# Turning output rows by a VectorE transpose of channel pairs, in a kernel of two attentions on one core

## The chip, the cores and the metric

The kernel runs on one NeuronCore of a Trainium2 chip. The metric is the time of one execution on the device, in microseconds (us), as the median of three runs. One further execution was recorded by the hardware profiler; its page and trace are what the document reads. Engines are named as the profile does: PE is TensorE's matmuls and PEld its loads of the stationary operand, DVE is VectorE, ACT is ScalarE, POOL is GpSimd, and SP issues the DMAs.

## What is computed

The input x has 2048 tokens of 512 channels. Two attentions run over it, and a gate g, one number for each token, mixes them.

```python
g = _sigmoid((x * gate_w).sum(-1, keepdims=True))
a = _A_ref(x, A_mem0, A_Wq, A_Wk, A_Wv, A_Wo, A_seg_len)
b = _B_ref(x, B_wq, B_wk, B_wv, B_wo, B_beta)
return g * a + (1 - g) * b
```

Branch A is a recurrence over 64 segments of 32 tokens. Eight memory rows stand in front of each segment; the 40 rows go through a masked attention with 32 heads of 128, and the output's first eight rows are the memory of the next segment.

```python
for s in range(n_seg):
    h = jnp.concatenate([mem, xs], axis=1)          # 8 + 32 rows
    q, k, v = (einsum('btd,dhe->bhte', h, W) for W in (Wq, Wk, Wv))
    p = _softmax(where(mask, q @ k.T * scale, -1e9))
    o = einsum('bhte,hed->btd', p @ v, Wo)
    mem = o[:, :M, :].copy()
    outs.append(o[:, M:, :])
```

Branch B is an attention with 32 heads of 16 over four chunks of 512 tokens, with a running memory matrix, and an output projection `wo`.

## The kernel before

The program is recorded first and emitted afterwards. `P.op` and `P.dma` append an instruction to an engine's list together with the named resources that it reads and writes, and each engine then runs its list in order and waits by semaphore for the other engines' last writers and readers of those resources. DMAs are all issued by SP, in the order in which they were recorded. So a place in the recording is a place in every queue.

At the start, `plan_loads` brings in x, the three weights of branch B (`wkB`, `wqB`, `wvB`, each 512 x 512 in four blocks of 128 channels), some small inputs, and the large weights of A. `x_chunk` turns x by identity matmuls on TensorE (line 573) into `xT`, channels on partitions. `gate_parts` turns the gate's weights by one more identity matmul (line 605) and computes g. Branch B's projections run in these first 50 us; its last chunk's projections come later, in small portions (`LateB`), with weight chunks loaded again by `ldc`.

After that `plan_a` runs sixteen groups of four segments. The order of the work in each group is written out by hand, in sixteen lists of tokens (`A_LIST0` to `A_LIST15`). `2.K0x` is a unit of segment 2, `bS`, `bE`, `bP`, `bT` are steps of branch B's attention, and units of the group before (`ol...`, `of`) and of still earlier groups (`tb`, `tf`) are mixed in. A tilde swaps ScalarE and VectorE for that copy, and a token with an `e` behind it is the copy that belongs to the unit. The projections are on line 1281, the scores on 1545 and 1550, the softmax sums on 1580, the values on 1610 and 1622, the output projection on 1368.

The output projection leaves four partial sums on four blocks of 32 partitions, in the f32 tile `WF` (`LNF` for the left-over rows). `fold` (line 1386) adds and turns them at once: a stationary operand of 32 channels from `WF` against a matrix `fold` of four stacked identities gives channels on partitions and tokens on columns. Of its result the first eight columns go to `hT` (the memory of the next segment, `hm`), and the others to the staging tile `aT_st` (`w_rows`, unit `ax`). Eight rows of each segment cannot be computed in the recurrence's place and come a group later: `ol_units` projects them, folds them (`of`) and copies them into `aT_st` as well (`ofe`). There are two such tiles, used by turns (`par`).

When a group's tile is whole, one DMA on line 1434 stores it to a scratch tensor `aTd` in DRAM, with channels still on partitions. Later `tail_units` loads it again into `aTg` (line 1452; the token `tl` issues the load once the store is recorded and branch B's rows are there). The unit `tb` projects branch B's rows (line 1463) and ScalarE scales them into `t1_sb`. The unit `tf` turns the reloaded rows by sixteen identity matmuls of 32 x 128 into a PSUM bank (line 1485), and its second half `tfe` has VectorE multiply by the gate, add `t1_sb` (line 1494) and SP store the output (line 1496). The last group skips scratch and is turned straight out of `aT_st`.

## Time and profile before

| what | value |
|---|---|
| median of three runs | 840.78 us (839.33 to 842.3) |
| the profiled execution's own time | 839.92 us |
| its span, from first to last instruction | 837.9 us |
| TensorE clock granted in it | 0.999 of full |
| packets moved, and of them under 512 B | 84442, 55296 |
| line 1485, ident x aTg, 240 matmuls | 6.3 us busy |
| line 1494, scale and add, 128 x 512, 15 times | 741 ns each |
| store of a group's rows (line 1434), 15 times | 128 KB, 1.8 us to landing |
| reload (line 1452), 15 times | 128 KB, 2.1 us to landing |
| output store (line 1496), 15 times | 128 KB, 1.9 us to landing |
| a group of four segments | some 48 us |

The span is what the profile shows of an execution; the time is 2 us longer than it, for what lies around it. A group row of the profile reads: line, engine, operation, tile written and tiles read, shapes, count; then busy time and the mean of one in ns; then the time that the engine was idle just before them, and what ended that. A timeline row reads: start, length, engine, line, operation, and in brackets the idle time before it and what ended it. Matmuls overlap with one another, so a row's length holds a drain that lies under the next work; the distance from start to start is what they cost.

### The profile page before, as it was taken

To read this page: it belongs to the slowest core of one execution; us is meant where nothing else is said; L and a number is where in the kernel's file an instruction comes from. 1 tells how busy PE (TensorE), PEld (TensorE's weight loads), DVE (VectorE), ACT (ScalarE), POOL (GpSimd) and SP (SyncE) were. 2 spreads that over 40 slices of the span, in tenths; PEclk is the share of its full clock that TensorE was granted. 3 is DMA by queue.
4 is the path that set the end of the run, shared out by engine and by line. 5 is a ranking of instruction groups with operands and counts; after the bars stand their busy time and mean duration, and the time that the engine had idled before them with its cause. 6 is when DMAs were issued, how large, how long until landed. Compare 5 with 4: busy or idle time off the path is not lost.

```text
span 837.9 us, 49436 instructions
## 1 busy us (share of the span) xinstructions
PE 808.7 (97%) x22174; PEld 438.8 (52%) x22174; DVE 572.1 (68%) x1381; ACT 589.7 (70%) x1506; POOL 284.6 (34%) x780
## 2 busy tenths in 40 slices
PE   8988999999999999999999999999999999999997
PEld 4544455555555555555555555555655555555554
DVE  4554656677676767766766767878688787777764
ACT  5546777677777777777687677677766677777544
POOL 3613233333333333333342333333333233434110
PEclk9999999999999999999999999999999999999999
DMA  9998212112011120111011020111112011110111
GB/s 318 419 362 243 62 41 61 47 31 62 16 30 41 25 55 27 46 38 46 23 46 39 24 56 25 47 39 40 35 25 61 17 49 32 40 41 15 30 41 47
DMA packets 84442, 57.50 MB, mean 69 GB/s; under 512 B 55296, under 2 KB 79112, under 8 KB 82696
## 3 DMA queue, kind: packets, MB, share of 16 engines
q1 hardware_dynamic: 84232, 54.36, 21.4%
q8 instruction: 174, 2.85, 1.4%
q14 instruction: 36, 0.29, 0.1%
HBM read 37.14 MB, written 17.20 MB: 65 GB/s over the span
## 4 chain that ended last, share of the span: by engine, by line
PE 87%; ACT 6%; DMA 3%; DVE 2%; issue 1%; SPq 1%; DVEq 0%; POOL 0%
PE ps L1281 46%; PE ps L1368 17%; PE ps L1386 3%; PE ps L1610 3%; PE ps L678 2%; PE ps L909 2%; PE ps L962 2%; PE ps L1463 2%; PE ps L1545 2%; PE ps L1580 1%; PE ps L696 1%; ACT PT L930 1%; ACT R_sb L1590 1%; ACT WF L390 1%; DMA wqB<-in_B_wq_dram 1%
## 5 line engine op out<-in xcount | busy, mean ns | idle before, releaser
L936 POOL TENSOR_SCALAR_AFFINE_SELECT PT<-PT 128x128 bf16<-128x128 bf16 (+2 forms) x320 | 117.5, 367 | 202.1 <-ACT PT L930 153.7
L930 ACT ACTIVATE PT<-ps 128x512 bf16<-128x512 f32 x320 | 174.9, 610 | 5.3 <-PE ps L909 4.2
L1281 PE MATMUL ps<-Wv_sb,hT 128*32 128x512 bf16 x2048 | 138.1, 379 | 0.0
L1281 PE MATMUL ps<-Wq_sb,hT 128*32 128x512 bf16 x2048 | 136.3, 379 | 0.4
L1281 PE MATMUL ps<-Wk_sb,hT 128*32 128x512 bf16 x2048 | 135.7, 379 | 0.5
L1368 PE MATMUL ps<-Wo_sb,OT_sb 128*32 128x512 bf16 x2048 | 129.5, 380 | 1.0 <-ACT OT_sb L390 0.6
L1600 POOL TENSOR_TENSOR P_sb<-P_sb,R_sb 128x64 bf16<-128x64 bf16 x128 | 51.0, 398 | 137.0 <-ACT R_sb L1590 131.2
L390 ACT ACTIVATE OT_sb<-ps 128x320 bf16<-128x320 f32 x170 | 68.6, 435 | 22.4 <-PE ps L1622 21.1
L1281 PEld LDWEIGHTS ps<-Wq_sb,hT 128*32 128x32 bf16 x2048 | 58.5, 97 | 46.6 <-ACT hT L390 2.9
L1281 PEld LDWEIGHTS ps<-Wk_sb,hT 128*32 128x32 bf16 x2048 | 58.8, 97 | 45.5 <-ACT hT L390 2.2
L390 ACT ACTIVATE WF<-ps 128x256 f32<-128x256 f32 x105 | 35.2, 381 | 55.3 <-PE ps L1368 53.0
L1368 PEld LDWEIGHTS ps<-Wo_sb,OT_sb 128*32 128x32 bf16 x2048 | 48.2, 96 | 45.5 <-ACT OT_sb L390 7.5
L1293 DVE STREAM_TRANSPOSE KT_sb<-KN_sb 128x256 f32<-128x256 f32 x128 | 56.5, 441 | 22.0 <-ACT KN_sb L390 19.0
L1293 DVE STREAM_TRANSPOSE QT_sb<-QN_sb 128x256 f32<-128x256 f32 x128 | 56.4, 441 | 21.8 <-ACT QN_sb L390 18.2
L390 ACT ACTIVATE QN_sb<-ps 128x512 bf16<-128x512 f32 x78 | 46.9, 604 | 33.3 <-PE ps L1281 32.7
L390 ACT ACTIVATE KN_sb<-ps 128x512 bf16<-128x512 f32 x75 | 45.0, 602 | 31.9 <-PE ps L1281 31.5
L1559 ACT ACTIVATE P_sb<-ps 128x224 bf16<-128x224 f32 x128 | 45.9, 359 | 28.5 <-PE ps L1550 20.4
L1281 PEld LDWEIGHTS ps<-Wv_sb,hT 128*32 128x32 bf16 x2048 | 50.0, 95 | 23.9 <-issue 0.6
L1594 DVE TENSOR_TENSOR P_sb<-P_sb,R_sb 128x160 bf16<-128x160 bf16 x128 | 42.3, 331 | 20.7 <-ACT R_sb L1590 18.5
L392 DVE CAST V_sb<-ps 128x512 bf16<-128x512 f32 x76 | 51.8, 682 | 5.5 <-PE ps L1281 5.1
L392 DVE CAST OT_sb<-ps 128x320 bf16<-128x320 f32 x86 | 41.1, 487 | 18.9 <-PE ps L1622 18.1
L1610 PEld LDWEIGHTS ps<-P_sb,V_sb 32*128 32x128 bf16 x2048 | 23.3, 91 | 57.5 <-DVE P_sb L1594 25.2
(142 smaller groups left out, 1488.6 us busy)
## 6 DMA issues: line engine op xcount, KB each, us to landing
Wk_sb<-in_A_Wk_dram SPq DMA_DIRECT2D x4, 1024.0 KB, 8.9
Wq_sb<-in_A_Wq_dram SPq DMA_DIRECT2D x4, 1024.0 KB, 12.4
Wv_sb<-in_A_Wv_dram SPq DMA_DIRECT2D x4, 1024.0 KB, 15.1
Wo_sb<-in_A_Wo_dram SPq DMA_DIRECT2D x8, 512.0 KB, 5.8
scr_vld<-VNL SPq DMA_DIRECT2D x16, 256.0 KB, 2.8
VL<-scr_vld SPq DMA_DIRECT2D x64, 64.0 KB, 2.6
scr_kqd<-stgk SPq DMA_DIRECT2D x12, 256.0 KB, 9.7
Vj<-scr_vd SPq DMA_DIRECT2D x32, 68.0 KB, 2.4
```

The costliest lines, as they stand in the source:

```text
L390: P.op("act", lambda a: a.activation(dst, src, ACT.Copy), reads=[v.rbank[k] for k in bks], writes=dres, name=name)
L392: P.op("dve", lambda d: d.tensor_copy(dst, src), reads=[v.rbank[k] for k in bks], writes=dres, name=name)
L930: P.op("act", lambda a: a.activation(pt, v.pb[bk], ACT.Exp, scale=v.SCALE_B), reads=[v.rbank[bk]], writes=[rp], name="be%d_%d" % (n, t))
L936: P.op("gp", lambda g: g.affine_select(mv, mv, [[0, len(cut)], [1, 128]], ALU.is_ge, 0.0, base=0, channel_multiplier=-1), reads=[rp], writ ...
L1281: ins = pe.matmul(pb[bk][SEG * j:SEG * (j + 1), :], lhs(c), cols(w, j) if split else w[:, 512 * j:512 * (j + 1)], start=(c == 0), stop=(c ...
L1293: P.op("dve", lambda d: d.transpose(to, src), reads=reads, writes=writes, name=name)
L1368: ins = pe.matmul(pb[bk][SEG * j:SEG * (j + 1), :], lhs(4 * k + j), Wo_sb[:, 4 * k + j, :], start=(first and k == ks[0]), stop=False, skip ...
L1386: ins = pe.matmul(pb[bk][SEG * j:SEG * (j + 1), SEG * n:SEG * (n + 1)], part[:, o:o + SEG], v.fold[:, :], start=True, stop=True, skip_grou ...
L1559: P.op("act", lambda a: a.activation(P_sb[:, b, :], pb[bk][:, 0:224], ACT.Exp, scale=SCALE), reads=[rbank[bk]], writes=[Rs("P%d" % b), Rs( ...
L1594: P.op("dve", lambda d: d.tensor_tensor(wide(P_sb, b)[:, :, 0:L], wide(P_sb, b)[:, :, 0:L], R_sb[:, b, :].rearrange("p (i q) -> p i q", q= ...
L1600: P.op(ENG["n"], lambda d: d.tensor_tensor(left(P_sb), left(P_sb), grp04(R_sb[:, b, :]), ALU.mult), reads=[Rs("R%d" % b)], writes=[Rs("P%d ...
L1610: ins = pe.matmul(pb[bks[j]][:, L * i:L * (i + 1)], V_sb[SEG * j:SEG * (j + 1), b, i * E:(i + 1) * E], P_sb[SEG * j:SEG * (j + 1), b, LW * ...
```

## The change

The rows of a group are now turned before they are stored. VectorE's transpose works on blocks of 32 x 32 words of 32 bits; a word here is a pair of neighbouring channels in bf16. For this the two channels of a pair have to lie beside each other in `aT_st`, so the assignment of channels to partitions changes in the whole kernel: partition p of block (h, n) now holds channel 256 h + 2 p + n instead of 128 c + p. What follows from that:

- B's weights are loaded in pieces of 2 KB (two neighbouring rows), A's weights with every second row to a block, and the weight chunks of `LateB` by two DMAs each.
- The gate's weights come straight into their place by a DMA of 256 pieces of 4 bytes; their turn on TensorE and its copy are gone. The load is issued behind x, and the gate's parts start two steps later.
- The identity matmuls that turn x and the first memory, and the fold, read their stationary operand with a step of two elements (`by_pairs`).
- The copies into `aT_st` write with a step of two bf16 elements (`a_rows`).

A new step `turn` stands where a new token `os` stands in the lists, once for each of the fifteen groups that go through scratch. It transposes the tile in place, and stores it with tokens on the rows by four DMAs, one for each block of 32 partitions, in pieces of 128 B. The store was recorded in `ofe` before; `os` stands some tokens behind it, in most cases near the start of the next list. Apart from `os`, the lists are the same. The reload brings rows of 1 KB with tokens on partitions, the identity matmuls of `tf` are gone for these fifteen groups, and line 1494 reads the reloaded tile in SBUF in place of a PSUM bank, and writes over it. The bank is still taken and given back. The last group keeps its sixteen matmuls, which now read with a step of two and write PSUM with a step of two.

```diff
-    dram("aTd", [NG, 128, C, 128])
+    dram("aTd", [NG, 128, DM])
...
-        ld("b" + nm, dst[:, :, :], src.rearrange("(c p) n -> p c n", p=128), nm + "B", "dma_" + nm)
+        ld("b" + nm, dst[:, :, :].rearrange("p (h n) m -> p h (n m)", h=2), src.rearrange("(h p n) m -> p h (n m)", h=2, n=2), nm + "B", "dma_" + nm)
...
+    P.dma(P.group("gw"), lambda s: s.dma_start(v.gw_sb[:, :].rearrange("p (h n) -> p h n", h=2), gate_w.rearrange("(h p n) -> p h n", h=2, n=2)), writes=[Rs("gw")], name="dma_gwr")
...
+class Pairs:
+    def __init__(self, ap):
+        self.ap = ap.rearrange("p (h t n) -> p h n t", h=2, n=2)
+
+    def __getitem__(self, key):
+        return self.ap[key[0], key[1] // 2, key[1] % 2, key[2]]
+
+
+def by_pairs(ap):
+    return Pairs(ap)
...
-                ins = pe.transpose(v.pb16[bk][:, o:o + 128], v.x_sb[:, i, c * 128:(c + 1) * 128], v.ident[:, :])
+                ins = pe.transpose(v.pb16[bk][:, o:o + 128], by_pairs(v.x_sb[:, i, :])[:, c, :], v.ident[:, :])
...
-    def weights():
-        bk = BK.take()
-        P.op("pe", lambda pe, bk=bk: pe.transpose(v.pb16[bk][:, 0:C], v.gwr_sb[0:C, :], v.ident[0:C, 0:C]),
...
+        for h in range(2):
+            P.dma(grp, lambda s, h=h: s.dma_start(dst[:, h], src[:, h]), writes=[Rs("woc%d" % (i % 4))] + ([Rs("wvB")] if i < 4 else []), name="ldc%d_%d" % (i, h))
...
-                    o = 256 * hf + 128 * n + SEG * j
-                    ins = pe.matmul(pb[bk][SEG * j:SEG * (j + 1), SEG * n:SEG * (n + 1)], part[:, o:o + SEG], v.fold[:, :],
+                    cols = by_pairs(part[:, :])[:, 2 * hf + n, SEG * j:SEG * (j + 1)]
+                    ins = pe.matmul(pb[bk][SEG * j:SEG * (j + 1), SEG * n:SEG * (n + 1)], cols, v.fold[:, :],
...
+    def a_rows(t):
+        return t[:, :, :].rearrange("p c t -> p (c t)").rearrange("p (a t c) -> p a t c", a=2, c=2)
...
-            stored.append(g)
-            P.dma(P.group("as%d" % g, "as%d" % par), lambda sp: sp.dma_start(v.aTd[g], aT_st[par][:, :, :]),
-                  reads=[Rs("aTl%d" % par)] + [Rs("aTx%d_%d" % (par, r)) for r in range(4)], writes=[Rs("aTd%d" % g)], name="sta%d" % g)
+            turns.append(turn)
+
+        def turn():
+            stored.append(g)
+            flat = aT_st[par][:, :, :].rearrange("p c t -> p (c t)")
+            turned = [Rs("aTl%d" % par)] + [Rs("aTx%d_%d" % (par, r)) for r in range(4)]
+            P.op("dve", lambda d: d.transpose(flat.bitcast(F32), flat.bitcast(F32)), writes=turned, name="aT%d" % g)
+            grp = P.group("as%d" % g, "as%d" % par)
+            rows = v.aTd[g].rearrange("(b t) (h j i) -> j t h b i", b=4, h=2, j=4)
+            for j in range(4):
+                P.dma(grp, lambda sp, j=j: sp.dma_start(rows[j], flat[SEG * j:SEG * (j + 1), :].rearrange("p (h b i) -> p h b i", h=2, b=4)),
+                      reads=turned, writes=[Rs("aTd%d" % g)], name="sta%d_%d" % (g, j))
...
             bk = B.take()
+            if not last:
+                return lambda: uf2(bk)
...
-                        ins = pe.matmul(pb[bk][q, c * 128:(c + 1) * 128], rows[:, c, q], ident[:, :], start=True, stop=True)
+                        ins = pe.matmul(by_pairs(pb[bk][q, :])[:, c, :], rows[:, c // 2, q, c % 2], ident[:, :], start=True, stop=True)
...
-                P.op("dve", lambda dv, c=c: dv.scalar_tensor_tensor(fin[:, c], pb[bk][:, c], g_sb[:, g:g + 1], t1_sb[:, c], ALU.mult, ALU.add),
+                P.op("dve", lambda dv, c=c: dv.scalar_tensor_tensor(fin[:, c], (pb[bk] if last else fin)[:, c], g_sb[:, g:g + 1], t1_sb[:, c], ALU.mult, ALU.add),
...
-            dst = aT_st[par][:, :, SEG * r:SEG * (r + 1) - M].rearrange("p (a c) t -> p a c t", a=2)
+            dst = a_rows(aT_st[par])[:, :, SEG * r:SEG * (r + 1) - M, :].rearrange("p a t c -> p a c t")
...
-    common = {"wl": wo_next, "bS": b_s, "bE": b_e, "bP": b_p, "bT": lambda: bat.run_late(1), "pj": late.project, "pp": late.finish}
+    common = {"wl": wo_next, "bS": b_s, "bE": b_e, "bP": b_p, "bT": lambda: bat.run_late(1), "pj": late.project, "pp": late.finish, "os": lambda: turns and turns.pop(0)()}
```

More of the change, by code (lines that the diff above doesn't have):

```diff
@@ L368, in over @@
     def over(home):
-        parts = {"mem0_sb": "mem0", "gwr_sb": "gwr", "beta_sb": "beta", "gB_sb": "gB", "omgB_sb": "omgB"}
+        parts = {"mem0_sb": "mem0", "beta_sb": "beta", "gB_sb": "gB", "omgB_sb": "omgB"}
         ops = []
@@ L415, in build @@
             v.late_const()
-        if n >= 36 and n % 2 == 0 and gates:
+        if n >= 38 and n % 2 == 0 and gates:
             gates.pop(0)()
@@ L601, in gate_parts @@
     st = {}
-    def weights():
-        bk = BK.take()
-        P.op("pe", lambda pe, bk=bk: pe.transpose(v.pb16[bk][:, 0:C], v.gwr_sb[0:C, :], v.ident[0:C, 0:C]),
-             reads=[Rs("gwr"), Rs("ident")], writes=[v.rbank[bk]], name="gwtr")
-        v.evac("dve", v.gw_sb[:, :], v.pb16[bk][:, 0:C], [bk], [Rs("gw")], "gwev")
-        BK.give(bk)
     def dots(k):
@@ L632, in f_m0tr @@
             for c in range(C):
-                ins = pe.transpose(v.pb16[bk][:, c * v.M:(c + 1) * v.M], v.mem0_sb[0:v.M, c * 128:(c + 1) * 128], v.ident[0:v.M, 0:v.M])
+                ins = pe.transpose(v.pb16[bk][:, c * v.M:(c + 1) * v.M], by_pairs(v.mem0_sb[0:v.M, :])[:, c, :], v.ident[0:v.M, 0:v.M])
             return ins
@@ L637, in memory @@
         BK.give(bk)
-    return [weights, memory] + [lambda k=k: dots(k) for k in range(NTT // 4)]
+    return [memory] + [lambda k=k: dots(k) for k in range(NTT // 4)]
 def b_projections(v):
@@ L1446, in tail_units @@
         last = g == ngrp - 1
-        rows = aT_st[g % 2] if last else aTg
+        rows = a_rows(aT_st[g % 2])
         rr = [Rs("aTl%d" % (g % 2))] + [Rs("aTx%d_%d" % (g % 2, r)) for r in range(4)] if last else [Rs("aTg")]
@@ L1451, in tail_units @@
         if not last:
-            P.dma(P.group("al%d" % g, "al"), lambda sp: sp.dma_start(aTg[:, :, :], v.aTd[g]), reads=[Rs("aTd%d" % g)], writes=[Rs("aTg")],
+            P.dma(P.group("al%d" % g, "al"), lambda sp: sp.dma_start(aTg[:, :, :].rearrange("p c t -> p (c t)"), v.aTd[g]), reads=[Rs("aTd%d" % g)], writes=[Rs("aTg")],
                   name="lda%d" % g, scratch=True)
@@ L1493, in uf2 @@
                 c = slice(h * 512 // n, (h + 1) * 512 // n)
[L1494 to L1495 removed]
+                P.op("dve", lambda dv, c=c: dv.scalar_tensor_tensor(fin[:, c], (pb[bk] if last else fin)[:, c], g_sb[:, g:g + 1], t1_sb[:, c], ALU.mult, ALU.add),
+                     reads=([rbank[bk]] if last else [Rs("aTg")]) + [Rs("g"), Rs("t1")], writes=([Rs("aTg")] if not h else []) + ([Rs("aTg%d" % h)] if n > 1 else []), name="fin%d_%d" % (g, h))
                 P.dma(g_out[g], lambda sp, c=c: sp.dma_start(out2d[g * 128:(g + 1) * 128, c], fin[:, c]), reads=[Rs("aTg%d" % h if n > 1 else "aTg")],
@@ L1700, in segment @@
         return units
-    stored, ended, pend = [], [], {}
+    stored, ended, pend, turns = [], [], {}, []
     st = {"tails": 0}
@@ L1795, in plan_a @@
         bat.run_late()
+        assert not turns
         while st["tails"] < ngrp or tail or pend:
```

142 lines of the change are left out of this document (70 added, 72 removed).

## The prediction

> **What bounds the kernel now.** I read the page's first and second parts, then the chain of waits, then every place in the timeline where the removed matmuls run.
>
> ```profile
> PE 808.7 (97%) x22174; PEld 438.8 (52%) x22174; DVE 572.1 (68%) x1381; ACT 589.7 (70%) x1506; POOL 284.6 (34%) x780
> ...
> DMA  9998212112011120111011020111112011110111
> GB/s 318 419 362 243 62 41 61 47 31 62 16 30 41 25 55 27 46 38 46 23 46 39 24 56 25 47 39 40 35 25 61 17 49 32 40 41 15 30 41 47
> ...
> PE 87%; ACT 6%; DMA 3%; DVE 2%; issue 1%; SPq 1%; DVEq 0%; POOL 0%
> ```
>
> TensorE is busy 97% of the span and is 87% of the chain that ends last, so work taken from it can shorten the span. DMA is full only in the first four slices of 21 us. VectorE has a third of the span free. The groups that the edit touches:
>
> ```profile
> L1386 PE MATMUL ps<-fold,WF 128*32 128x32 f32 x2048 | 36.9, 199 | 4.4 <-ACT WF L390 2.1 <-ACT hT L390 0.7 <-DVE oTt L986 0.2
> ...
> L1293 DVE STREAM_TRANSPOSE KT_sb<-KN_sb 128x256 f32<-128x256 f32 x128 | 56.5, 441 | 22.0 <-ACT KN_sb L390 19.0
> ...
> L1545 PEld LDWEIGHTS ps<-QT_sb,KT_sb 128*32 128x32 bf16 x2048 | 31.9, 95 | 28.3 <-DVE QT_sb L1293 10.8 <-DVE KT_sb L1293 8.0 <-issue 1.2
> ...
> L1386 PEld LDWEIGHTS ps<-fold,WF 128*32 128x32 f32 x2048 | 30.7, 111 | 21.5 <-ACT WF L390 8.8 <-DVE WF L392 2.0 <-ACT aT_st L390 1.3
> L1485 PE MATMUL ps<-ident,aTg 128*32 128x128 bf16 x240 | 6.3, 219 | 0.3 <-issue 0.3
> ```
>
> (busy us and mean ns, then idle before). The 240 matmuls of L1485 are what goes; the 6.3 us counts drains that lie under the next work. Start to next start is what counts, and what follows:
>
> ```profile
> 414.63 0.40 PE L1485 MATMUL ps<-ident,aTg 128*32 128x128 bf16 x16
> 414.96 0.27 PE L1610 MATMUL ps<-P_sb,V_sb 32*128 32x40 bf16 x16
> ...
> 808.49 0.40 PE L1485 MATMUL ps<-ident,aTg 128*32 128x128 bf16 x16
> 809.15 0.61 PE L1386 MATMUL ps<-fold,WF 128*32 128x32 f32 x32 [0.26 <-ACT WF L390]
> ```
>
> At 414.63 TensorE could have gone on to the values matmuls, whose operand was ready. At 808.49 the sixteen matmuls only fill a wait for ScalarE's copy of WF.
>
> **The change, part by part.**
>
> *Matmuls removed.* Fifteen groups lose 16 each. In the timeline such a group holds TensorE 0.22 us where the next instruction is ready (827.07 to 827.29, 317.97 to 318.19): 15 x 0.22 = 3.3 us at most. I went through all fifteen. Two give the whole 0.22 (414.63, 743.22). Seven give 0.05 to 0.14, because a softmax mask, a WF copy or VectorE's own L1494 becomes the limit that much earlier. Six fill a wait and give nothing (271.00, 354.89, 597.81, 645.37, 808.49, 820.12). That is about 1.0 us. The chain of waits is kinder: it passes through L1485 in twelve of the fifteen, 2.9 us together. Bounds 0 and -3.3; I take the middle of the two counts, **-1.9 us**.
>
> *Turn added.* Fifteen VectorE transposes of 128x256 words, 441 ns each by the L1293 row: 6.6 us. Each stands at `os`, in thirteen cases at the start of a segment's projections, where VectorE idles until TensorE has finished them: at 169.63 its first copy of Q had waited 0.89 us. All that the turn reads was written before that point. Queued behind it is that first copy, for which the next transpose and the scores wait. Cover gone, it would cost up to 6.6 us; I take **0**, which is the lower bound too, as nothing comes earlier for it.
>
> *L1494* (the final scale and add, 741 ns) now reads the reloaded rows from SBUF. The nearest SBUF-only row is L980, the same operation at 706 ns: up to 0.5 us over fifteen, mostly off the path. 0. It now waits for the reload by itself; behind it on VectorE stand softmax scalings that TensorE waits for (at 827.07, the one at 828.76).
>
> *Store in four.* One store of 128 KB in 128 pieces of 1 KB becomes four DMAs, together 1024 pieces of 128 B.
>
> ```profile
> VL<-scr_vld SPq DMA_DIRECT2D x64, 64.0 KB, 2.6
> ...
> scr_aTd<-aT_st SPq DMA_DIRECT2D x15, 128.0 KB, 1.8
> ```
>
> (KB each, median us to landing.) The trace has no store in pieces under 1 KB. The nearest row in piece count is the VL load, 256 pieces of 256 B, 2.6 us, with issues on SP of about 0.6 us. Four give 2.4 us of issues and a landing about 5.5 us after `os`, with the turn. Bounds for the last landing: 1.8 us (the old store) and 4 x 2.6 = 10.4 us (one after the other). The staging buffer is written again only some 11 us after the group's start (L1434 at 264.20, first rows of the next use at 276.98), so the cover holds up to about 8 us from `os`. SP's loads behind it are late by about 2 us; TensorE waited for such loads 2 us in the whole span. Only at the end is it tight:
>
> ```profile
> 823.17 0.32 SPq L1452 DMA_DIRECT2D aTg<-scr_aTd  x1
> ...
> 828.09 0.75 DVE L1494 SCALAR_TENSOR_TENSOR aTg<-ps,g_sb,t_sb 128x512 bf16<-128x512 f32 x1
> ```
>
> The last stored group's turn can begin only after the WF copy that ends at 820.75, so it ends at 821.2; four issues last to 823.6; a landing of 2.6 is then 826.2, past the store of output 13 (issue 0.34, landing 1.9: 825.8), which also has to leave aTg. The reload goes out at 826.2 and lands, at 2.1, at 828.3; L1494 wants it at 828.09. That is **+0.2 us**, which I take; store landings of 1.8 to 10.4 us make it 0 to 8. [...]
>
> *Loads.* The three B weights come in 2 KB pieces: 1536 become 768. The price of a piece from part 3 of the page: queue q1 took 21.4% of 16 x 837.9 us = 2869 us for 84232 packets and 54.36 MB; at the best slice's 419 GB/s the bytes alone take 2075 us, the rest is 9.4 ns a packet. Two weights' 512 fewer are 0.3 us over 16 engines, and TensorE's idle 0.35 us before 9.22 waits for wqB. The gate's load in 256 tiny pieces gives 0.15 us back, later, in the full-DMA stretch. **-0.3 us**, bounds +0.2 and -0.5. The late weight chunks in two DMAs each add eight SP issues of some 0.5 us between 80 and 150 us; nothing on TensorE waits for them: 0, at most 1.
>
> *Gate transpose gone:* one matmul, 0.10 us on the chain at 37.34: **-0.1 us**.
>
> *Strided reads.* The x transposes' stationary operand now steps two bf16 (4 bytes). L1545 already loads such a step, 95 ns against 96 for the dense L1368: 0; upper bound, if the 56 ns pitch of L573 doubled, 64 x 56 = 3.6 us. The fold's stationary now steps two f32 (8 bytes), which no row shows. Sixteen fold matmuls start within 0.12 us, 7.5 ns each; 2560 of them are 19 us, and half the load rate would add up to that. Bounds 0 and +19; I take 0, by the nearest row, L1545. [...] Copies into aT_st now write every second bf16; at 210 ns for 48 columns they are nearly all fixed cost: 0.
>
> **Sum** against the profiled execution (839.92 us, span 837.9): -1.9 + 0 + 0.2 - 0.3 - 0.1 = -2.1, so 837.8 and a span of 835.8. The median shown, 840.78, lies 0.86 above that execution; the same step from it gives **838.7 us**.
>
> **Rivals.**
> 1. *All slots count* (every 0.22 us, loads 0.5, gate 0.1, no tail): -3.9, 836.9. For it: the chain runs through twelve. Against: the waits after six.
> 2. *Hidden anyway*: 1.0 us of slots and 0.4 of start, given back as 0.2 at the tail and small delays behind the turns: about -0.4, 840.4. For it: the count by hand.
> 3. *Late reload and uncovered turns* (slower): VectorE holds L1494 until the reload lands, and the scaling behind it holds TensorE. Every us of store landing past 2.4 at the end is a us of span; with 5 us that is +2.6, and half of the turns uncovered is +3.3: 840.78 - 2.3 + 5.9 = 844.4. It decides once landing passes 4 us and cover fails at half the groups. Against: VectorE's idle before the first copies, 14.8 us over 17 of them.
> 4. *Fold reads at half rate* (slower): 7.5 ns becomes up to 15, half of it to all on the path: 838.7 + 10 to 19, 848 to 858. Decides once the pitch passes 9.5 ns (2560 x 2 = 5 us).
> 5. The edit doing nothing can be left out: the changed program's instruction order lacks the fifteen sets of matmuls.
>
> **How the numbers follow.** Forecast 0.47 (837.0 to 840.3), rival 1 0.10, rival 2 0.15, rival 3 0.16, rival 4 0.12. 0.3% of 840.78 is 2.5 us, about what a measurement here can tell from nothing, so faster means under 838.3: all of rival 1 and somewhat over half of the forecast, 0.36. Within: the rest of it and rival 2, 0.36. Slower: rivals 3 and 4, 0.28. The range 836 to 846 leaves out rival 4 and some of rival 1.
>
> **What would show it.** L1485 at 16 matmuls, TensorE's busy time down by about 3 us, its idle up by 1. Fifteen more VectorE transposes at 441 ns with the first Q copies no later. A fold pitch of 7.5 ns and a 113 ns load. The last reload landing before 828. The prediction is wrong if the fold's load is longer, if TensorE waits for VectorE behind L1494, or if the gap at 9.2 us stays.

## The result, and the profile after

The changed kernel takes 842.48 us (median of 20 executions; 841.75 to 844.24) where the kernel before took 841.72 (20 more of it; 839.33 to 842.38). The medians are 0.8 us apart, the means (842.69 and 841.37) 1.3 us; the ratio is 1.0015, 95% interval 1.0009 to 1.0021. The kernel is slower by some 1.3 us, 0.15% of its time, and 2.1 us less had been forecast. The profiled execution took 841.9 us, its span is 839.7.

The page of the changed kernel, parts 1, 3 and 4 (busy time, share and instructions of each engine; queue, packets, MB, share; the chain that ended last):

```profile
PE 806.0 (96%) x21927; PEld 431.3 (51%) x21933; DVE 576.5 (69%) x1395; ACT 590.3 (70%) x1506; POOL 286.1 (34%) x780
...
q1 hardware_dynamic: 98016, 54.36, 22.2%
q8 instruction: 172, 2.82, 1.4%
...
PE 84%; ACT 6%; DMA 4%; DVE 3%; issue 1%; SPq 1%; DVEq 0%; ACTq 0%
```

TensorE did get its work taken away: 808.7 us of busy time became 806.0. But its idle time, span less busy, rose from 29.2 to 33.7 us. So the question is not whether the matmuls are gone, but what TensorE waits for in their place. The share of DMA in the chain went from 3 to 4%. The groups that answer to those shown before:

```profile
L1396 PE MATMUL ps<-fold,WF 128*32 128x32 f32 x2048 | 36.9, 199 | 5.3 <-ACT WF L390 2.6 <-ACT hT L390 0.7 <-DVE oTt L996 0.2
L1396 PEld LDWEIGHTS ps<-fold,WF 128*32 128x32 f32 x2048 | 30.8, 111 | 23.5 <-ACT WF L390 10.6 <-DVE WF L392 2.0 <-ACT aT_st L390 1.3
L1453 DVE STREAM_TRANSPOSE aT_st<-aT_st 128x256 f32<-128x256 f32 x15 | 6.4, 429 | 0.0
L1511 PE MATMUL ps<-ident,aT_st 128*32 128x128 bf16 x16 | 0.6, 304 | 0.0
L1520 DVE SCALAR_TENSOR_TENSOR aTg<-aTg,g_sb,t_sb 128x512 bf16<-128x512 bf16 x15 | 11.1, 742 | 2.3 <-ACT V_sb L390 1.8 <-ACT t_sb L1495 0.6
```

The fold is unharmed: 199 ns a matmul and 111 ns a load, before and after, although its stationary operand now steps 8 bytes. The turn (L1453) costs 429 ns, fifteen times, with no idle ahead of it. The last group's sixteen identity matmuls, which now step in PSUM and in the stationary operand, went from 219 to 304 ns. L1520 is as long from SBUF (742 ns) as it was from PSUM (741), and has one idle stretch of 1.8 us. That one stands at the end. The timeline of the changed kernel there:

```profile
821.08 0.42 DVE L392 COPY WF<-ps 128x256 f32<-128x256 f32 x1 [1.75 <-ACT WF L390]
821.42 0.43 DVE L1453 STREAM_TRANSPOSE aT_st<-aT_st 128x256 f32<-128x256 f32 x1
821.88 3.03 SPq L1457 DMA_DIRECT2D scr_aTd<-aT_st  x4
824.96 0.60 SPq L1522 DMA_DIRECT2D out_dram<-aTg  x1
826.94 0.33 SPq L1476 DMA_DIRECT2D aTg<-scr_aTd  x1
830.48 0.75 DVE L1520 SCALAR_TENSOR_TENSOR aTg<-aTg,g_sb,t_sb 128x512 bf16<-128x512 bf16 x1 [1.76 <-ACT V_sb L390]
831.15 0.32 DVE L1620 TENSOR_TENSOR P_sb<-P_sb,R_sb 128x160 bf16<-128x160 bf16 x1
831.61 0.28 PE L1636 MATMUL ps<-P_sb,V_sb 32*128 32x40 bf16 x16 [1.01 <-DVE P_sb L1620]
```

Read it from the bottom. TensorE waits 1.01 us for the softmax scaling; the scaling stands on VectorE behind L1520; L1520 stands 1.76 us idle. The brackets name ScalarE's V_sb copy, but that one started at 829.78 and has nothing to do with L1520's operands. What L1520 reads is the reload, issued at 826.94 and landed 3.4 us later. In a second trace of the changed kernel (e8 below) the bracket names that reload:

```profile
832.35 0.75 DVE L1520 SCALAR_TENSOR_TENSOR aTg<-aTg,g_sb,t_sb 128x512 bf16<-128x512 bf16 x1 [1.61 <-DMA aTg<-scr_aTd]
```

To compare executions, count from the WF copy: the reload goes out at +5.86 us and L1520 runs at +9.40. In the kernel before the WF copy ran at 820.33, and the same two were at +2.84 and +7.76. Output 13's store, which has to leave aTg before the reload may write it, goes out at +3.88 now and went out at +1.11 before:

```profile
820.33 0.42 DVE L392 COPY WF<-ps 128x256 f32<-128x256 f32 x1 [1.75 <-ACT WF L390]
821.44 0.34 SPq L1496 DMA_DIRECT2D out_dram<-aTg  x1
```

To see where along the span time comes and goes, the starts of the 128 score exponentials of the recurrence (ACT, `P_sb<-ps`) are compared between two traces. From 100 us to the last of them at 826 the changed kernel is +0.92 us behind, and behind it, in the tail, another +1.10. A second trace of the changed kernel has +2.12 and +0.95; a second one of the kernel before has +2.99 and +0.70 against its first, 0.9 us of that tail a single stall of the kind shown below. So but for that stall the tail is steady, and the middle moves by 1 to 3 us from one execution to the next. What moves it is the subject of the third group of experiments.

### The profile page after: what moved, and what is told of

Its sections match the earlier page's. It is cut to its first block, busy times and chain, and to the rows that moved or that the text cites. A ratio compares the mean times of both kernels' runs of the same rounds, so it can differ in the third digit from the quotient of the medians.

```text
span 839.7 us, 49011 instructions
## 1 busy us (share of the span) xinstructions
PE 806.0 (96%) x21927; PEld 431.3 (51%) x21933; DVE 576.5 (69%) x1395; ACT 590.3 (70%) x1506; POOL 286.1 (34%) x780
## 3 DMA queue, kind: packets, MB, share of 16 engines
q8 instruction: 172, 2.82, 1.4%
## 4 chain that ended last, share of the span: by engine, by line
PE 84%; ACT 6%; DMA 4%; DVE 3%; issue 1%; SPq 1%; DVEq 0%; ACTq 0%
PE ps L1291 45%; PE ps L1378 17%; PE ps L1396 3%; PE ps L1636 3%; PE ps L919 2%; PE ps L686 2%; PE ps L972 2%; DMA scr_mzd<-MZ 2%; PE ps L1571 2%; PE ps L1487 1%; PE ps L1606 1%; ACT PT L940 1%; ACT R_sb L1616 1%; ACT WF L390 1%; PE ps L704 1%
```

## The experiments

### The tail: is it the place of the turn, or the store?

e1 moves one token, so that the last stored group's turn stands ahead of VectorE's WF copy.

```diff
-    2.v0 2.L1 2.n1 tb 2.N1 ... 2.W0a 2.E0b 2.oL 2.W0b 2.H0 2.H1~ os pl0x
+    2.v0 2.L1 2.n1 tb 2.N1 ... 2.W0a 2.E0b 2.oL 2.W0b os 2.H0 2.H1~ pl0x
```

> The last of the fifteen turns is moved ahead of the two copies of WF, to where VectorE stands idle from 819.3 us on; nothing else moves. Theory A (the end of the run holds the loss: turn at 821.4, four store issues of 0.76 us, the output store and the last reload one behind the other, so that the scale and add starts at 830.48 where it could have started some 0.5 us behind the one of before plus 0.7): the reload goes out about 1.5 us earlier, the 1.76 us of idle time on VectorE shrink to under 0.5, and the time falls by 0.9 to 1.2 us against the changed kernel. Theory B (what was lost is lost in the groups, to fifteen turns on VectorE and to single stalls of TensorE; the end only shows it): within 0.3 us of the changed kernel.

840.45 us; ratio to the kernel before 1.0002 (0.999 to 1.0015). The same spot of its timeline:

```profile
820.77 0.43 DVE L1453 STREAM_TRANSPOSE aT_st<-aT_st 128x256 f32<-128x256 f32 x1
821.24 2.58 SPq L1457 DMA_DIRECT2D scr_aTd<-aT_st  x4
822.61 0.42 DVE L392 COPY WF<-ps 128x256 f32<-128x256 f32 x1 [1.40 <-ACT WF L390]
826.90 0.33 SPq L1476 DMA_DIRECT2D aTg<-scr_aTd  x1
830.30 0.75 DVE L1520 SCALAR_TENSOR_TENSOR aTg<-aTg,g_sb,t_sb 128x512 bf16<-128x512 bf16 x1
832.07 0.27 PE L1636 MATMUL ps<-P_sb,V_sb 32*128 32x40 bf16 x16
```

From the WF copy the reload is now at +4.29 and L1520 at +7.69, without idle time, and the values matmuls wait for nothing. The tail is -0.27 us against before: 1.35 us come back. The turn itself costs as much as it did (0.43 us in both timelines); it only no longer stands behind a copy that waits 1.75 us for ScalarE.

e2 keeps the place and takes the four stores away: one DMA of 128 rows of 1 KB, which leaves the output's rows out of place.

```diff
-            rows = v.aTd[g].rearrange("(b t) (h j i) -> j t h b i", b=4, h=2, j=4)
-            for j in range(4):
-                P.dma(grp, lambda sp, j=j: ...
+            P.dma(grp, lambda sp: sp.dma_start(v.aTd[g], flat), reads=turned, writes=[Rs("aTd%d" % g)], name="sta%d" % g)
```

> The turn stays, but each group is stored by one DMA of 128 pieces of 1 KB, so the rows of these groups stand in the wrong places of the output. Theory A (late last reload): one issue of 0.4 us and a landing of 1.8 us bring the reload back to where it was wanted, about 1.0 us less than the changed kernel. Theory C (the 1024 small pieces or the 3 us of issues on SP also cause the 1.1 us stall of TensorE at 694.28, where the store was issued at 693.34): that stall goes as well, about 2 us less. Theory B (turns and stalls that have nothing to do with the store): no change within 0.3 us.

840.75 us, 1.0004 (0.9989 to 1.0019), tail -0.24. e5 takes the turn's transpose away and leaves the four stores (rows out of place):

```diff
-            P.op("dve", lambda d: d.transpose(flat.bitcast(F32), flat.bitcast(F32)), writes=turned, name="aT%d" % g)
```

> The changed kernel without its fifteen transposes (the store in four and all else stay; the rows of these groups come out of place). Read in the trace against the changed kernel from 100 us on, since the first 90 us vary by 2 us from one execution to the next. If the turns are covered, as forecast: no step of over 0.1 us at any turn, and at most 0.4 us at the end, where the turn stands ahead of the last store; the time stays within 0.5 us of the changed kernel. If half of them lie open (rival 3): about 3 us less.

840.44 us, 0.9995 (0.9983 to 1.0008), tail -0.28. So taking away either half is enough: with a quick store the late turn is harmless, and with an early start the slow store is. Their sum, behind a late copy, is what reaches the end. Against each other the traces show no step at the other fourteen turns, apart from the fetch stalls described below.

A third thing goes with the reload's 3.4 us. It took 3.0 and 3.1 in the two other traces with this order of work (e8 and e15, below), but 2.0 and 1.9 in e4 and e7 (below), which have the same late turn and four stores. What differs is the place of a 16 KB packet of queue q8, whose kind the page calls "instruction": 172 of them in the changed kernel, some 1.1 us each (1.4% of 16 x 839.7 us). They are called fetches here; that they carry TensorE's instructions is an estimate, worked out below. In the first three traces one starts 1.19, 0.75 and 0.63 us after the reload's issue, in the other two over 3 us after it. The 300 reloads of the 20 traces agree. The 78 with a fetch starting 0.45 to 1.25 us behind the issue took 2.7 to 4.1 us, 3.1 at the median; the 159 with no fetch from 1.1 us ahead of the issue to 1.25 us behind it took 2.04 at the median (1.85 to 4.05). The same reload near 700 us in two traces of the changed kernel took 2.05 us with a fetch at 1.64 us and 3.52 with one at 0.89. In the first trace of the kernel before one reload of fifteen meets a fetch in that stretch, in the first of the changed kernel seven, and the median of the fifteen goes from the first of these lines to the second:

```profile
aTg<-scr_aTd SPq DMA_DIRECT2D x15, 128.0 KB, 2.1
...
aTg<-scr_aTd SPq DMA_DIRECT2D x15, 128.0 KB, 2.9
```

Had the last reload landed in 2.0 us, L1520 would have run at about +8.0 in place of +9.40, 0.3 us behind e1's. That is an estimate from these times; no run moved that fetch alone.

e10 is e1 with one more turn taken apart from its store: at the head of the list of group 12, where group 11's rows are turned, the store now stands behind the second K projection. It asks whether that store's issue is what stalls TensorE there (see below).

```diff
-    os 0.K1x 0.K0x tfe 0.K0y bE bE 0.k0~ 0.Q0x 0.Q0y bE 0.K1y 0.qt ...
+    oT 0.K1x 0.K0x tfe 0.K0y bE bE 0.k0~ 0.Q0x 0.Q0y bE 0.K1y oS 0.qt ...
...
```

> As the kernel with the last turn moved ahead, and the four store issues of group 11, recorded at the head of group 12, come some tokens later (about 4 us); TensorE's and VectorE's order is untouched. In both traces with the four issues at that place TensorE stood still for 1.0 us inside its first eight matmuls of the group (694.28 and 695.83), 0.7 us beyond the end of a 16 KB fetch of its own instructions; in the one with a single store issue it did not. If the four issues or their small pieces hold up that fetch: the stall goes, and the time falls by 1.0 us against the kernel with the last turn moved ahead, to 0.7 us under the kernel before. If the stall belongs to the place in TensorE's instruction stream alone: it stays at the same instruction.

840.11 us, 1.0002 (0.9988 to 1.0017). The tail is mended as in e1 (-0.27), and the stall stayed (0.80 us): the store is not its cause.

The changed kernel and e1 were run once more on one chip.

> The changed kernel itself once more, on the same chip and beside the same runs of the kernel before as the two below. If its loss is the late end (1.1 us beyond 826 us in the first trace), less some 0.5 us for the matmuls: 0.3 to 0.9 us over the kernel before, and again 1.0 to 1.4 us lost between 826 us and the end, while the single stalls of TensorE inside a run of matmuls come at some of the same places with other lengths.

> The kernel with the last turn moved ahead, once more, for a narrower interval. The end theory: 0.9 to 1.4 us under the changed kernel run beside it, and 0.2 to 0.8 us under the kernel before. If the end is not the cause: no difference to the changed kernel.

843.5 us, 1.0018 (1.0005 to 1.0031), against 841.69, 1.0000 (0.9985 to 1.0015). The tail is settled: it is +0.95 to +1.10 us in the three traces with the late turn (the changed kernel, e8, e15) and -0.24 to -0.29 in the nine with the moved token (e1, e10 to e12, e14, e16 to e19). So 1.0 to 1.35 us are lost there, by which of the two they are counted from, and one token gets them all back.

### The slots: what were the 240 matmuls worth?

e3 is the channel layout alone: no turn, the store at its old place in one DMA, and the identity matmuls back behind the reload. In the layout of pairs they step by two elements in both operands.

```diff
-            turns.append(turn)
+            stored.append(g)
+            flat = aT_st[par][:, :, :].rearrange("p c t -> p (c t)")
+            P.dma(P.group("as%d" % g, "as%d" % par), lambda sp: sp.dma_start(v.aTd[g], flat), ...
...
-        rows = a_rows(aT_st[g % 2])
+        rows = a_rows(aT_st[g % 2] if last else aTg)
...
-            if not last:
-                return lambda: uf2(bk)
...
-                P.op("dve", lambda dv, c=c: dv.scalar_tensor_tensor(fin[:, c], (pb[bk] if last else fin)[:, c], ...
+                P.op("dve", lambda dv, c=c: dv.scalar_tensor_tensor(fin[:, c], pb[bk][:, c], ...
```

> The new assignment of channels with everything that it brings at the start (B's weights in 2 KB pieces, the gate's load, strided stationary operands), but rows stored as before, in one DMA as soon as they are whole, and turned by sixteen identity matmuls behind the reload; no turn on VectorE. Theory A: 0.3 to 0.5 us under the kernel before (0.4 at the start, 0.1 for the gate, strided reads free). A rival, that the strided reads or the strided copies cost something in every group: 0 to 2 us over the kernel before.

843.32 us, 1.0037 (1.0022 to 1.0051). That is not the price of the layout, as e6 shows: e3 with the matmuls' operands dense as they were before, which leaves the channels out of order.

```diff
-                        ins = pe.matmul(by_pairs(pb[bk][q, :])[:, c, :], rows[:, c // 2, q, c % 2], ident[:, :], start=True, stop=True)
+                        if last:
+                            ins = pe.matmul(by_pairs(pb[bk][q, :])[:, c, :], rows[:, c // 2, q, c % 2], ident[:, :], start=True, stop=True)
+                        else:
+                            ins = pe.matmul(pb[bk][q, c * 128:(c + 1) * 128], aTg[:, c, q], ident[:, :], start=True, stop=True)
```

> As the kernel with the layout alone, but its 240 identity matmuls have the dense operands of the kernel before (the channels of fifteen groups come out of order). In the former kernel sixteen of them took 0.61 us in the place of 0.40, and it stood 2.3 us behind the kernel before between 110 and 826 us. If that came from their strided reads and strided PSUM columns: 0 to 0.4 us in that stretch now, and a time 0 to 0.5 us under the kernel before. If it came from another part of the layout (the fold's stride of 8 bytes, the copies with a stride): still 2 us or more behind.

841.28 us, 1.0009 (0.9996 to 1.0022). The groups of e3, then of e6:

```profile
L1511 PE MATMUL ps<-ident,aTg 128*32 128x128 bf16 x240 | 9.3, 304 | 0.0
L1511 PEld LDWEIGHTS ps<-ident,aTg 128*32 128x32 bf16 x240 | 6.2, 117 | 2.1 <-ACT R_sb L1613 0.3 <-issue 0.2 <-ACT aT_st L390 0.2
```

```profile
L1514 PE MATMUL ps<-ident,aTg 128*32 128x128 bf16 x240 | 6.1, 219 | 0.0
L1514 PEld LDWEIGHTS ps<-ident,aTg 128*32 128x32 bf16 x240 | 4.6, 96 | 2.1 <-ACT R_sb L1616 0.3 <-issue 0.2 <-ACT aT_st L390 0.2
```

From the first one's start to the next instruction's, where that is ready, sixteen of them hold TensorE 0.39 us with the steps and 0.22 without, 2.6 us in fifteen groups. A matmul takes 304 ns for 219, a load 117 for 96; the result in PSUM and the stationary operand both step, and no run parts the two.

e4 and e7 put the matmuls back into the changed kernel, with their result in a bank that nothing reads; e4 with steps (shown), e7 dense, by the lines of e6 as well.

```diff
-        rows = a_rows(aT_st[g % 2])
+        rows = a_rows(aT_st[g % 2] if last else aTg)
...
-            if not last:
-                return lambda: uf2(bk)
```

> The changed kernel with the sixteen identity matmuls put back behind each reload, into the bank that is taken anyway and that nobody reads; so all of the change is there but the removal. The difference to the changed kernel is the worth of the 240 matmuls. By my count in the timeline 1.0 us, by the offsets of the two traces in the groups 0.6, by the chain of waits 2.9; the prediction took 1.9. Under 1.2 says that the count of the ready followers was the right view, over 2.4 that the chain was.

> The changed kernel with sixteen matmuls back behind each reload, now with the dense operands of the kernel before, into the bank that nobody reads. Between 110 and 826 us, apart from single stalls of TensorE inside a run of matmuls, it falls behind the changed kernel by the worth of the 240 matmuls: 0.6 us by the offsets of the two first traces, 1.0 by my count of ready followers, 1.9 by the forecast, 2.9 by the chain of waits.

845.94 us, 1.0069 (1.0055 to 1.0082), and 843.18 us, 1.0031 (1.0019 to 1.0044). Against the changed kernel's 1.0015 to 1.0018 the dense ones cost 0.0013 to 0.0016 of the time, 1.1 to 1.3 us, where each set fills 0.22 us of a full TensorE, 3.3 in all. The intervals leave about 1.2 us to either side of that.

The traces say the same from the other side. For each interval between two segments' exponentials from 100 us on, take the shorter of two traces, so that what strikes only one of them falls out: over all pairs of twelve traces with the whole change, the moved token in some of them, the sum is 0.80 us below that of the two traces before, with a spread of 0.8. The intervals that differ from both of them in three quarters of the twelve, leaving out those where a stall of the next part lies, are -0.16 us (at 318), -0.14 (722), -0.11 (735), five of -0.05 to -0.09, and three losses of +0.05 to +0.11, the largest at 508, in all -0.5. So the slots are worth 0.5 to 0.8 us, net of whatever else the change does in the middle, near the count by hand.

### What moves the middle: stalls behind the fetches of queue q8

The largest single step in the groups is at 694 us. Three engines of the changed kernel:

```profile
693.22 0.22 ACT L390 ACTIVATE aT_st<-ps 128x48 bf16<-128x48 f32 x1
694.28 0.55 PEld L1291 LDWEIGHTS ps<-Wk_sb,hT 128*32 128x32 bf16 x15 [0.98 <-issue]
694.28 1.05 PE L1291 MATMUL ps<-Wk_sb,hT 128*32 128x512 bf16 x16 [1.11 <-ACT PT L940]
```

The load says "issue": nothing that the profile shows held it. The matmul names the PT exponential, for which the program does not wait there; it waits for the hT copy, which ended at 693.32. What does stand beside such gaps is the fetches of queue q8, 172 of 16 KB each (2.82 MB by 172). In 20 traces, from 100 to 826 us, there are 34 gaps of 0.24 us or more inside a run of one projection's matmuls on the rows of a segment. 32 of them end 1.0 to 1.75 us after the end of one of these fetches, a stretch that covers 16% of the time; the other two are of 0.24 and 0.25 us. Counted in the program's order, a bf16 matmul with its load as two, the instruction that resumes is the 191st to 197th after a multiple of 256. 16 KB by 256 is 64 bytes an instruction; 49011 instructions of the page by 64 are 3.14 MB, and the two instruction queues moved 3.12. TensorE's own 43860 matmuls and loads by 64 are 2.81 MB, and q8 moved 2.82. From these numbers I estimate that a fetch brings 256 of TensorE's instructions, and that TensorE now and then reaches the end of what has been fetched; no view shows what it waits for in these gaps. (Runs of the fold are left out of this count, as most of their gaps wait for a copy of WF, at the same place in every trace.)

e11 tests that: e1 with 64 small matmuls in place of four of the nine that run ahead of all work, which adds 120 instructions and moves every boundary.

```diff
-        for n in range(WARM):
+        for n in range(WARM - 4):
+        for n in range(64):
+            ins = pe.matmul(v.pb[bk][0:32, 0:32], v.warm[:, 0:32], v.warm[:, 0:32], start=True, stop=True)
```

> As the kernel with the last turn moved ahead, but TensorE's warm-up holds 64 matmuls of 32 columns in the place of 4 of 512, 120 instructions more ahead of all else. In all nine traces so far a stall inside a run of matmuls ended 1.3 to 1.6 us after the end of a 16 KB fetch of TensorE's instructions, and always at an instruction whose number leaves 194 to 197 when divided by 256. If the fetch is the cause, every stall lies at 194 to 197 again in the new count, which are other instructions than before: none at the eighth part of the first K projection of group 12 (0.8 and 1.07 us in three traces) and others, up to 1 us each, elsewhere. If a stall belongs to its place in the program (bank, semaphore, store): it is where it was. The time: within 1 us of the kernel with the last turn moved ahead, either side.

The stall at the group 12 projection is gone, and others stand at instructions that had none in any other trace (323.8, 383.6, 415.8, 456.9, 516.1 us), at the same remainder. One of them in e11's timeline, in the middle of a run of one projection:

```profile
323.26 0.38 PE L1293 MATMUL ps<-Wq_sb,xL 128*32 128x512 bf16 x2
323.27 0.20 PE L1398 MATMUL ps<-fold,WF 128*32 128x32 f32 x1
323.78 0.61 PE L1293 MATMUL ps<-Wq_sb,xL 128*32 128x512 bf16 x6
```

The time is 842.67 us, 1.001 (0.9999 to 1.0021); e11 also adds the small matmuls. Taken over a trace from 90 us on, such stalls come to 2.0 us in the first trace of the kernel before, 3.1 and 3.5 in two of the changed kernel, and 1.0 to 4.2 in the others of its order. The kernel before was profiled again:

> The kernel before, for a second trace of it. If the stalls at instruction fetches are not the change's: it has some 3 to 6 of them, 0.3 to 1 us each, at numbers that leave 194 to 197, and at other places than the changed kernel, whose count of instructions differs.

844.57 us, span 842.5, and 5.8 us of stalls. This is one execution, slower than the other 29 of that kernel on the same chip (839.38 to 843.7). So the stalls are not a property of the change: which boundary stalls depends on the order, how long depends on the execution. Only the one at 694 us (0.3 to 1.1 us, in eight of the thirteen traces with the changed kernel's order on TensorE and not in the two of the kernel before) might be put down to it. What holds TensorE there stays open.

### The start: two side effects of the layout

In every trace of the new layout so far ScalarE's first late V_sb copy waited near 61 us, and TensorE behind it; in none before. The changed kernel:

```profile
60.74 0.60 ACT L390 ACTIVATE V_sb<-ps 128x512 bf16<-128x512 f32 x1 [1.28 <-DMA scr_mzd<-MZ]
61.39 0.40 PE L972 MATMUL ps<-PT,Vj 128*32 128x256 bf16 x8 [0.57 <-ACT V_sb L390]
```

The change drops a tile of 256 B (`gwr_sb`) from SBUF, so what lies behind it moves: the memory states MZ from byte 19408 to 19152, into V_sb's later place (17152 to 19200). V_sb must now wait until MZ has been stored. e14, e15 and e16 are e1, the changed kernel and e10 with the tile put back, unused; e17 is e1.

```diff
-          ... ("mem0_sb", [128, DM], BF16, 0), ("beta_sb", [128, HB], BF16, 0),
+          ... ("mem0_sb", [128, DM], BF16, 0), ("gwr_sb", [128, 128], BF16, 0), ("beta_sb", [128, HB], BF16, 0),
```

> The kernel of e1 (last turn ahead of the WF copy) with the 256 B array put back, unused, at its old place in the SBUF: no instruction changes, only addresses. Theory (the moved addresses cost the layout part 0.3 to 0.5 us): the V_sb copy near 60 us no longer waits for the scr_mzd store (1.0 to 1.7 us in all traces of the new layout), the first V matmul of the four waits under 0.1 us for it, and the time is 0.3 to 0.5 us under that of e17: ratio to before about 0.9995. Rival (the wait is absorbed by what follows, since the kernel before waits 0.6 us for t_sb a microsecond later): the wait goes and as much appears behind it; time equal to e17, ratio 1.0000.

> The changed kernel with the 256 B array put back at its old place, and nothing else. Theory: the wait near 60 us goes, the tail's 1.1 to 1.35 us stay: about 1.0 us over before, ratio 1.0011. Rival: ratio 1.0017 as the changed kernel had.

> The kernel of e10 (last turn ahead of the WF copy, group 12's store behind its second K projection) with the 256 B array put back. Theory: 0.3 to 0.5 us under before, 839.7 to 840 on a chip where before has 840.3, ratio 0.9995. Rival: equal to before, ratio 1.0002 as e10 had.

> e1 once more, on the chip of e14: the wait of the V_sb copy is there again (1.0 to 1.7 us), ratio to before 1.0000 to 1.0002 as twice before.

841.57 us, 1.001 (0.9996 to 1.0024); 842.24, 1.0011 (0.9996 to 1.0027); 840.63, 0.9996 (0.9982 to 1.001); and 841.99 for e17, 1.0008 (0.9992 to 1.0025). e15's ratio is the 1.0011 of the theory, but its interval holds the rival's 1.0017 as well, and e14 and e17, which differ by the tile alone, are alike. The wait goes with the tile put back, in all three. But in e14 TensorE's next wait grows by more than the 0.57 us saved (in e15 it is 0.37 us, in e16 under 0.15). In e14's timeline:

```profile
59.72 0.63 ACT L390 ACTIVATE V_sb<-ps 128x512 bf16<-128x512 f32 x1
61.14 0.40 PE L972 MATMUL ps<-PT,Vj 128*32 128x256 bf16 x8
62.56 1.05 PE L823 MATMUL ps<-woB_sb,xT 128*32 128x512 bf16 x16 [1.01 <-ACT t_sb L390]
```

From the scores at 57 us to the softmax sums at 65 it takes 8.0 and 8.15 us in the two traces before, 7.7 to 8.3 with the moved places in all but two (9.9 and 10.2, from other waits), and 7.3, 7.8 and 8.4 with the old ones. My theory fell: the moved address shifts a wait and costs nothing that shows.

The other side effect does cost. The interval between two exponentials at 97 us is 2.37 and 2.33 us before, and 2.41 to 3.67, median 2.7, in sixteen traces of the new layout. SP's issues of the kernel before, then of the changed one, ahead of it:

```profile
92.42 0.37 SPq L789 DMA_DIRECT2D woB_sb<-in_B_wk_dram  x1
93.53 0.34 SPq L840 DMA_DIRECT2D scr_kqd<-aTg  x1
93.91 0.43 SPq L877 DMA_DIRECT2D QTj<-scr_kqd  x1
94.38 1.84 SPq L877 DMA_DIRECT2D KTj<-scr_kqd  x4
```

```profile
91.83 1.22 SPq L799 DMA_DIRECT2D woB_sb<-in_B_wk_dram  x2
93.09 1.36 SPq L850 DMA_DIRECT2D scr_kqd<-aTg  x1
94.49 0.43 SPq L887 DMA_DIRECT2D QTj<-scr_kqd  x1
94.97 1.83 SPq L887 DMA_DIRECT2D KTj<-scr_kqd  x4
...
97.05 0.40 PE L919 MATMUL ps<-QTj,KTj 32*128 32x256 bf16 x8 [0.45 <-DVE KN_sb L392]
```

The weight slice that the layout splits into two DMAs takes SP 1.22 us in place of 0.37, and the store behind it 1.36 in place of 0.34, so QTj goes out 1.2 us later against the work around it (the changed trace runs some 0.6 us ahead there) and the scores wait for it. The bracket names a copy here; in e17, where the wait is 1.29 us, it names the QTj load:

```profile
99.08 0.40 PE L919 MATMUL ps<-QTj,KTj 32*128 32x256 bf16 x8 [1.29 <-DMA QTj<-scr_kqd]
```

e18 and e19 (from e1 and e10) issue this one slice behind the Vj load; no other queue changes its order.

```diff
...
-            for n in range(4 if k == 3 else k > 3):
-                self.load()
+            if k == 3:
+                for n in range(4):
+                    self.load()
+            elif k == 4:
+                self.put_off += 1
+            elif k > 4:
+                self.late_loads()
+                self.load()
...
+        if job > 0:
+            v.late_b.late_loads()
```

> The kernel of e1 with one of the eight B-weight slice loads (the one at 92 to 93 us, two DMAs) issued behind the Vj load instead of ahead of the scr_kqd store and the QTj and KTj loads; every other queue keeps its order. Theory (two issues in place of one on SP delay QTj, and PE waits for it): QTj's issue comes 1.2 us earlier against the late segments, L919's wait near 97 us (0.45 to 1.29 us in traces of the new layout, none in the kernel before) goes, the interval of the segment exponentials there is 2.3 to 2.4 us, and the time is 0.3 to 0.5 us under e1's: ratio to before 0.9997. Rival (L919 waits for the KN and KT copies or for something that comes at the same time anyway): the interval stays at 2.6 us or more.

> The same move in the kernel of e10 (last turn ahead of the WF copy, group 12's store behind its second K projection). Theory: the same interval of 2.3 to 2.4 us, ratio to before 0.9995 or a little less. Rival: interval 2.6 us or more, ratio 1.0000.

In e18's trace the scores wait for nothing:

```profile
92.87 0.33 SPq L864 DMA_DIRECT2D scr_kqd<-aTg  x1
93.24 0.98 SPq L901 DMA_DIRECT2D QTj<-scr_kqd  x1
...
96.49 0.40 PE L935 MATMUL ps<-QTj,KTj 32*128 32x256 bf16 x8
```

The interval is 2.33 us in both, as before: 0.3 to 0.5 us typically, up to 1.3, lay here. Their profiled spans, 836.5 and 836.9 us, are the shortest of all versions that compute the whole result, with 1.5 and 1.0 us of fetch stalls. The times do not bear that out: 840.64 us, 1.0009 (0.9996 to 1.0023), and 841.14 us, 1.0013 (0.9998 to 1.0029). So the slice's cost is shown in the traces and not in a time; half a microsecond is less than these intervals can tell. No version here beats the kernel before by what can be measured.

## Why the prediction was wrong

*The tail term, +0.2, was mis-sized; it is +1.0 to +1.35.* That the last reload holds VectorE, and VectorE TensorE, was seen rightly. What failed is the sentence "lands, at 2.1": the reload landed 3.4 us after its issue (3.0 and 3.1 in e8 and e15), and by the 300 reloads above (3.1 us at the median with a fetch 0.45 to 1.25 us behind the issue, 2.04 with none near) the likely cause is a fetch that fell into it; 2.0 held in e1, e4 and e7. The sum had no term for such fetches. Counted from the WF copy in the frame of the kernel before, the reload was forecast for 826.2 and went out at 826.19, but this match is luck in part. The forecast has the reload wait for the last of the four stores. In the trace that store had landed at +5.19; the four issues took 3.03 us for the 2.4 assumed, output 13's store stood behind them in SP's queue, and the reload waited for this one, landed at +5.84. The upper bound of 8 was far off. Of rival 3 the hold on VectorE and TensorE at the end happened, by the reload and not by the stores' landing; its uncovered turns did not. That small pieces by themselves make a store land later was not shown: the 128 B pieces' stores land in 2.5 us at the median, where the 1 KB pieces' landed in 1.8, but no slower than the VL load's 2.7, and no run separates the pieces from the four issues.

*The slots term, -1.9, was too large; it is -0.5 to -0.8 by the traces, and -1.1 to -1.3 by e7.* The step that failed is "the middle of the two counts". The hand count (1.0) was close; the chain of waits (2.9) names what ran last at each step, not what would come next in its place.

*The SP term, "nothing on TensorE waits for them: 0, at most 1", was wrong in its value and right in its bound:* 0.3 to 0.5 us at 97 us in the traces, by queueing on SP.

*Start.* B's weights give 0.15 to 0.2 us (the first gap between the weights' projections is 1.38 us in both traces before, near 1.2 after), not 0.3; the gate's 0.1 was not measured by itself. The first 100 us differ by 0.8 to 1.1 us between traces of one kernel, and by 2.8 over the twelve, so neither shows in a time.

*Fold 0, turns 0, L1520 0, strided x transposes 0:* right. Rival 4 fell with the 199 and 111 ns. Of the signs of being wrong that the prediction names, one came: TensorE waits behind L1520.

*Sum.* -0.65 (slots) + 1.2 (tail) + 0.4 (slice) - 0.25 (start) is +0.7 us; the ratio's interval is 0.8 to 1.8. Without the tail it would be -0.5; e1 has 1.0002, 1.0000 and 1.0008 in three measurements. About half a microsecond to one stays open, with the tail and without it. The fetch stalls vary by more than that (1.0 to 5.8 us in a trace), but no run shows that they make it up.

## What to carry to other kernels

Count what matmuls taken out of a full engine are worth by what follows them, instruction by instruction; here that count, 1.0 us, was nearer than the chain's 2.9 to the 0.5 to 0.8 of the traces. A step that moves in front of a DMA is to be costed to the landing of the last transfer that depends on it, at its end of the kernel, and placed ahead of any copy that waits for another engine; here 1.0 to 1.35 us hung on a place behind a copy that waited 1.75. Give that landing a range and not one number: here the same 128 KB took 2.0 or 3.4 us, by where a fetch of 16 KB fell. A layout that splits a DMA into two puts every later DMA of that queue behind one more issue (here 1.22 us of SP in place of 0.37, and QTj out 1.2 us later): look at what is queued behind it, not at who waits for the split load itself.

## What was not expected of the hardware

- TensorE stood 0.25 to 1.1 us at a time inside runs of matmuls with ready operands, labelled "issue" on the weight load and with a wrong releaser on the matmul; 1 to 6 us in an execution of 840. Of the 34 counted above in 20 traces 32 ended 1.0 to 1.75 us after the end of a 16 KB packet of queue q8, at the 191st to 197th instruction after a multiple of 256. That TensorE had run out of fetched instructions there is an estimate from these numbers.
- Such a packet goes with slower loads: a reload of 128 KB took 3.1 us in place of 2.04, at the median, where one started 0.45 to 1.25 us after its issue.
- A matmul that writes PSUM in steps of two f32 from a stationary operand in steps of two bf16 took 304 ns for 219.
- A store issue of 32 KB in pieces of 128 B took SP 0.61 us at the median in the changed kernel's trace, and 0.76 in the mean of the last four, where one of 128 KB in pieces of 1 KB took 0.33 before. Half a weight slice took 0.61 us, where the whole one, in pieces of 256 B as well, had taken 0.37 to 0.56; and the issue behind was longer in that trace (1.36 for 0.34 us behind the weight slice at 92 us, 0.60 for 0.34 behind the last four stores).
